# Feed-forward matmuls as pairs on two 64-row tiles, in a fused attention and gated feed-forward kernel

## The chip, the cores and the metric

The kernel runs on one core of one Trainium2 chip. The metric is device time in microseconds (us), the median of several executions.

Engine names in the profile: PE is TensorE, PEld its weight loads, DVE VectorE, ACT ScalarE, POOL GpSimd, SP the engine whose queue issues most of the DMAs.

## The reference

```
attention: 8 batches, 16 query heads, 4 key/value heads, 384 positions, head size 64
  a = softmax(q k^T / 8);  x = a v,  laid out as [batch, 384, 1024]
feed-forward with a spatial gate:
  h = relu(x @ w_in)                 # 1024 -> 1024
  u, v = halves of h                 # 512 each
  v_n = (v - mean) / sqrt(var + 1e-6)
  v_s = w_spatial @ v_n + b_spatial  # along the 384 positions
  out = (u * v_s) @ w_out            # 512 -> 1024
```

## The kernel before

The kernel is a software pipeline over the eight batches. While batch b has its scores and exps and v chunks 0 and 1, batch b-1 has v chunk 2, its spatial and u chunks and o (output) chunk 0, and batch b-2 has o chunks 1 to 5. The order on every engine is the order of the program.

- A *score unit* is two matmuls on two 64-row tiles of TensorE, since the head size is 64, and one exp over 1024 columns. 18 units make a batch.
- A *value* (three per batch) is 36 matmuls on four 32-column tiles.
- *v*, *u*, *sp* (spatial) and *o* (output) chunks are ordinary matmuls with 128 rows: 3 v chunks of 8 matmuls, 4 u of 8, 4 sp of 3, 6 o of 4 per batch. TensorE writes their sums into PSUM; four of its banks are used in rotation, and in this program the next chunk waits until VectorE or ScalarE has read its bank out.

```
def score_mm(b, u):
    for half in range(2):
        lo, hi = half * D, (half + 1) * D          # D = 64
        nc.tensor.matmul(sc[:, half, :], kT[b][lo:hi, gp, t, :], rhs[lo:hi, :], start=True, stop=True)

def u_mm(b, mu):
    pu = ps.tile([P, 512], FP32, ...)              # four PSUM banks in rotation
    for kc in range(NKT):
        nc.tensor.matmul(pu[:, 0:S], w_in16[:, kc, mu*P:(mu+1)*P], xT[b][:, kc, :], ...)

def visit(b, vi):                                  # nine visits per batch
    score_mm(b, 2*vi); score_mm(b, 2*vi + 1)
    exp(b, 2*vi)
    ...
    if vi == 4:
        norm(c); exp(b, u1)
        o_mm(d, 5); o_copy(d, 5)                   # the copy is followed by the store, on SP's queue
        v_mm(b, 0); relu(b, 0); stats(b, 0)
    ...

def next_loads(b, vi):                             # b is the next batch here
    if vi == 0: ...                                # loads on SP, casts on GpSimd
    if vi == 5: dma_transpose_k(b); dma_transpose_q(b, 0)
    if vi == 6: dma_transpose_q(b, 1)
```

The keys and queries of the next batch are transposed by DMAs from SBUF to SBUF, which SP issues.

The softmax here doesn't subtract the row's maximum and nothing guards it: scores larger than these inputs give would overflow.

Of the kernel before, what the change touches and what calls it, by code (L numbers as in the profile page):

```python
# [10 lines left out]
FP32 = mybir.dt.float32  # L11
# [8 lines left out]
def kernel(  # L20
# [20 lines left out]
    P = 128  # L41
# [23 lines left out]
    att_a = ctx.enter_context(tc.tile_pool(name="att_a", bufs=2))  # L65
# [8 lines left out]
    ps = ctx.enter_context(tc.tile_pool(name="ps", bufs=4, space=bass.MemoryType.PSUM))  # L74
# [13 lines left out]


# [102 lines left out]
    def transpose_ws(st):  # L192
        ws16 = loaded["ws16"]
        psw = ps.tile([P, NST, P], FP16, name=f"psw_{st}", tag="ps")
        for tt in range(NST):
            nc.tensor.transpose(psw[:, tt, :], ws16[:, tt, st, :], ident16)
        nc.vector.tensor_copy(wsT16[:, st, :].rearrange("p (t q) -> p t q", t=NST), psw)
# [23 lines left out]
    def transpose_k(b, gp):  # L221
        k16 = loaded["k16", b]
        pk = ps.tile([P, NST, P], FP16, name=f"pk_{b}_{gp}", tag="ps")
        for t in range(NST):
            nc.tensor.transpose(pk[:, t, :], k16[:, gp, t, :, :].rearrange("p h d -> p (h d)"), ident16)
        if b not in kT:
            new_kT(b)
        nc.vector.tensor_copy(kT[b][:, gp], pk)

    def transpose_q(b, gp, qt):  # L230
        q16 = loaded["q16", b, gp]
        if (b, gp) not in qT:
            new_qT(b, gp)
        pq = ps.tile([P, G, P], FP16, name=f"pq_{b}_{gp}_{qt}", tag="ps")
        for j in range(G):
            nc.tensor.transpose(  # L236
                pq[:, j, :], q16[:, qt, j, :, :].rearrange("p h d -> p (h d)"), ident16
            )
        nc.vector.tensor_copy(qT[b, gp][:, qt], pq)  # L239
# [4 lines left out]
    def score_mm(b, u):  # L244
        qt, gp, t = u // 6, (u % 6) // 3, u % 3
        sc = ps_sc.tile([P, 2, 512], FP32, name=f"sc_{b}_{u}", tag="sc")
        rhs = qT[b, gp][:, qt].rearrange("p j q -> p (j q)")
        for half in range(2):
            lo, hi = half * D, (half + 1) * D
            nc.tensor.matmul(  # L250
                sc[:, half, :], kT[b][lo:hi, gp, t, :], rhs[lo:hi, :], start=True, stop=True
            )
        held["sc", b, u] = sc
# [7 lines left out]
    def value_mm(b, qt):  # L261
# [15 lines left out]
        sums = ps.tile([P, 512], FP32, name=f"sums_{b}_{qt}", tag="ps")  # L277
        tiles(sums, lambda t, g: ones32)
        held["sums", b, qt] = sums
        for jj in range(2):  # L280
            X = ps.tile([P, 512], FP32, name=f"X_{b}_{qt}_{jj}", tag="ps")
            tiles(X, lambda t, g: v16[:, g, t, 32 * jj : 32 * (jj + 1)])
            held["X", b, qt, jj] = X

# [20 lines left out]
    def v_mm(b, st):  # L305
        pv = ps.tile([P, 512], FP32, name=f"pv_{b}_{st}", tag="ps")
# [45 lines left out]
    def sp_mm(b, m, dst=None):  # L352
        if dst is None:
            dst = ps.tile([P, 512], FP32, name=f"psp_{b}_{m}", tag="ps")
# [20 lines left out]
    def u_mm(b, mu):  # L375
        pu = ps.tile([P, 512], FP32, name=f"pu_{b}_{mu}", tag="ps")
# [22 lines left out]
    def o_mm(b, i):  # L399
        tt, half = i // 2, i % 2  # L400
        po = ps.tile([P, 512], FP32, name=f"po_{b}_{tt}_{half}", tag="ps")
# [26 lines left out]


# [76 lines left out]
    def next_loads(b, vi):  # L506
        if vi == 0:
            load_k(b)
            load_q(b, 0)
            load_q(b, 1)  # L510
            load_v(b)
            for gp in range(NGP):
                cast_k(b, gp, nc.gpsimd)
            for gp in range(NGP):
                for half in range(2):
                    cast_q(b, gp, 0, NST, half, nc.gpsimd)
            cast_v(b, nc.gpsimd)
        if vi == 5:
            dma_transpose_k(b)
            dma_transpose_q(b, 0)  # L520
        if vi == 6:
            dma_transpose_q(b, 1)

    def visit(b, vi):
        c, d = b - 1, b - 2
        u0, u1 = 2 * vi, 2 * vi + 1
        score_mm(b, u0)
        score_mm(b, u1)
        exp(b, u0)
        if vi == 0:  # L530
            value_mm(c, 2)
            rec(c, 2)
            exp(b, u1)
            xmul(c, 2)
            if d >= 0:
                o_mm(d, 1)
                o_copy(d, 1)
        if vi == 1:
            exp(b, u1)
            if d >= 0:  # L540
                for i in (2, 3):
                    o_mm(d, i)
                    o_copy(d, i)
            else:
                for gp in range(NGP):
                    transpose_q(1, gp, 1)
                v_mm(0, 1)
                relu(0, 1)
                stats(0, 1)
        if vi == 2:  # L550
            exp(b, u1)
            v_mm(c, 2)
            relu(c, 2)
            stats(c, 2)
            if d < 0:
                for gp in range(NGP):
                    transpose_q(1, gp, 2)
                cast_ws()
        if vi == 3:
            value_mm(b, 0)  # L560
            rec(b, 0)
            exp(b, u1)
            rstd(c)
            xmul(b, 0)
            if d >= 0:
                o_mm(d, 4)
                o_copy(d, 4)
            else:
                for st in range(NST):
                    transpose_ws(st)  # L570
        if vi == 4:
            norm(c)
            exp(b, u1)
            if d >= 0:
                o_mm(d, 5)
                o_copy(d, 5)
            v_mm(b, 0)
            relu(b, 0)
            stats(b, 0)
        if vi == 5:  # L580
            exp(b, u1)
            for m in range(NDT):
                sp_mm(c, m)
                sp_add(c, m)
            u_mm(c, 0)
            gate(c, 0)
        if vi == 6:
            value_mm(b, 1)
            rec(b, 1)
            exp(b, u1)  # L590
            xmul(b, 1)
            u_mm(c, 1)
            gate(c, 1)
        if vi == 7:
            exp(b, u1)
            for mu in (2, 3):
                u_mm(c, mu)
                gate(c, mu)
        if vi == 8:
            exp(b, u1)  # L600
            v_mm(b, 1)
            relu(b, 1)
            stats(b, 1)
            o_mm(c, 0)
            o_copy(c, 0)

    def tail():
        c, d = B - 1, B - 2
        value_mm(c, 2)
        rec(c, 2)  # L610
        rstd(c, 0, 2)
        xmul(c, 2)
        for i in (1, 2):
            o_mm(d, i)
            o_copy(d, i)
        norm(c, 0, 2)
        v_mm(c, 2)
        relu(c, 2)
        stats(c, 2)
        rstd(c, 2, 3)  # L620
        norm(c, 2, 3)
        for i in (3, 4, 5):
            o_mm(d, i)
            o_copy(d, i, nc.scalar)
# [16 lines left out]
    with tc.manual_schedule(engines={PE, POOL, SP, DVE, ACT}):  # L641
        first_batch()
        for b in range(1, B):
            for vi in range(VISITS):
                visit(b, vi)
                if b + 1 < B:
                    next_loads(b + 1, vi)
        tail()
# [29 lines left out]
```

## Time and profile before

265.06 us (three runs, 265.05 to 265.34).

| what | read from | value |
|---|---|---|
| PE busy share | the page | 94% |
| one batch in the steady part | timeline, from value to value | 29.47 us |
| 512-column matmul, start to start | instruction starts | 0.216 us |
| 384-column matmul, start to start | instruction starts | 0.162 us |
| extra gap where the tiling mode changes | instruction starts | 0.093 to 0.106 us, and 0.01 behind it |

The head of the page of the kernel before: busy us, share of the span, number of instructions. Below it is the head of the part on the chain that ended last.

```profile
span 262.5 us, 4805 instructions
PE 245.9 (94%) x1957; PEld 103.2 (39%) x1957; DVE 140.6 (54%) x261; ACT 187.3 (71%) x241; POOL 43.6 (17%) x69
...
PE 86%; ACT 8%; DVE 2%; DMA 1%; issue 0%; ACTq 0%
```

A piece of the timeline of the kernel before. Columns: start in us, duration in us, engine, line, operation, result <- inputs, tile rows*columns, shapes, number of instructions merged.

```profile
121.63 0.60 PE L250 MATMUL sc<-qT,kT 64*128 64x512 f16 x4
...
122.17 1.90 PE L403 MATMUL po<-w_out,gT 128*128 128x512 f16 x8
...
124.00 0.60 PE L250 MATMUL sc<-qT,kT 64*128 64x512 f16 x4
```

Compare starts, not durations, because matmuls are pipelined. From 122.17 to 124.00 eight matmuls pass: 8 x 0.216 = 1.73, and 0.10 more for the change back to the scores' mode. From 121.63 to 122.17 there are two pairs, 2 x 0.22 and again 0.10. Counted over a batch: 27.26 us of matmul slots (24 v + 24 o + 27 value + 18 score slots of 0.216; 32 u + 12 sp of 0.163) and 21 mode changes of about 0.10. That leaves almost nothing of the 29.47.

The DMA transposes of the kernel before, in the same view (SPq is SP's queue, the duration is that of the issue), and the first score of the batch that needs them:

```profile
104.03 1.40 SPq L209 DMA_TRANSPOSE kT<-k  x1
105.53 3.94 SPq L216 DMA_TRANSPOSE qT<-q  x2
...
118.07 0.61 PE L250 MATMUL sc<-qT,kT 64*128 64x512 f16 x4
```

The last of them had landed at 111.7 by the DMA's completion events, over six us before the score.

### The profile page before, as it was taken

The numbers are of one execution on the slowest core, as the hardware profiler recorded it, in microseconds if no ns is written. First come the engines' busy times: TensorE is split into PE (matmuls) and PEld (weight loads), VectorE is DVE, ScalarE is ACT, GpSimd is POOL, SyncE is SP. The second block draws the span as 40 slices with busy tenths as digits, with TensorE's granted clock in tenths as the row PEclk, the third lists the DMA queues.
The fourth block names the chain that finished last, engine by engine and source line by source line (L and its number), as shares of the span: only waits on it lengthen the run. The fifth ranks groups of instructions, "written<-read, shape, count | busy, mean of one in ns | idle before, by whom it ended". The sixth has DMA issues, their size and how long they took to land.

```text
span 262.5 us, 4805 instructions
## 1 busy us (share of the span) xinstructions
PE 245.9 (94%) x1957; PEld 103.2 (39%) x1957; DVE 140.6 (54%) x261; ACT 187.3 (71%) x241; POOL 43.6 (17%) x69
## 2 busy tenths in 40 slices
PE   2787798999999999999999999999999999999794
PEld 1233343443344333443344333443344333444351
DVE  2326649626493356626483457636483457637452
ACT  2889888667957888668957888668957888663301
POOL 2707422000160014100330016000330000000000
PEclk9999999999999999999999999999999999999998
DMA  8999999931997069902994079902985031002306
GB/s 185 283 254 352 275 230 74 172 14 60 303 263 128 0 215 340 198 2 70 305 278 100 4 217 339 195 0 76 314 264 100 2 160 54 28 0 84 160 0 240
DMA packets 57430, 41.60 MB, mean 158 GB/s; under 512 B 26816, under 2 KB 53568, under 8 KB 57408
## 3 DMA queue, kind: packets, MB, share of 16 engines
q1 hardware_dynamic: 53648, 37.89, 54.1%
q0 software_dynamic: 2720, 3.15, 8.4%
q10 hardware_dynamic: 1040, 0.26, 0.4%
q8 instruction: 15, 0.25, 0.4%
q14 instruction: 7, 0.06, 0.1%
HBM read 25.95 MB, written 12.58 MB: 147 GB/s over the span
## 4 chain that ended last, share of the span: by engine, by line
PE 86%; ACT 8%; DVE 2%; DMA 1%; issue 0%; ACTq 0%
PE po L403 17%; PE pu L378 16%; PE pv L308 16%; PE sc L250 14%; PE X L269 10%; PE sums L269 7%; ACT aT L259 6%; PE psp L356 5%; DMA q<-in_q_dram 1%; DVE v_s L368 1%; ACT rec L288 1%; PE sc_sp L356 1%; ACT rec L287 1%; PE pq L236 1%; DVE qT L239 1%; DVE ws L187 1%
## 5 line engine op out<-in xcount | busy, mean ns | idle before, releaser
L259 ACT ACTIVATE aT<-sc 128x1024 f16<-128x1024 f32 x144 | 140.8, 1019 | 40.9 <-PE sc L250 40.9
L250 PE MATMUL sc<-qT,kT 64*128 64x512 f16 x288 | 46.6, 394 | 5.7 <-ACT aT L259 4.4
L296 DVE TENSOR_TENSOR xt<-X,rec 128x512 f16<-128x512 f32 x48 | 30.9, 686 | 32.3 <-PE X L269 25.4
L403 PE MATMUL po<-w_out,gT 128*128 128x512 f16 x192 | 47.4, 380 | 0.0
L308 PE MATMUL pv<-w_in,xt 128*128 128x512 f16 x192 | 45.5, 380 | 0.0
L378 PE MATMUL pu<-xt,w_in 128*128 128x384 f16 x256 | 45.5, 327 | 0.0
L329 DVE BATCH_NORM_STATS2 stats<-v_r 128x6 f32<-128x512 f32 x24 | 16.7, 694 | 39.4 <-ACT v_r L322 39.3
L269 PE MATMUL X<-aT,v 128*32 128x512 f16 x576 | 35.5, 381 | 0.0
L421 DVE COPY osb<-po 128x512 f32<-128x512 f32 x42 | 28.6, 683 | 7.1 <-PE po L403 7.1
L378 PEld LDWEIGHTS <-w_in 128*128 128x128 f16 x256 | 23.9, 98 | 20.8 <-issue 5.9
L159 POOL CAST q<-q 128x768 f16<-128x768 f32 (+2 forms) x32 | 24.2, 785 | 41.4 <-DMA q<-in_q_dram 31.2
L390 DVE SCALAR_TENSOR_TENSOR gT<-pu,v_s 128x384 f16<-128x384 f32 x32 | 17.8, 558 | 17.6 <-PE pu L378 16.5
L308 PEld LDWEIGHTS <-xt 128*128 128x128 f16 x192 | 17.4, 98 | 25.0 <-issue 6.4
L403 PEld LDWEIGHTS <-gT 128*128 128x128 f16 x192 | 16.6, 98 | 26.2 <-issue 9.3
L250 PEld LDWEIGHTS <-kT 64*128 64x128 f16 x288 | 10.7, 94 | 34.3 <-issue 30.4
L140 POOL CAST k<-k 128x384 f16<-128x384 f32 x13 | 6.3, 507 | 106.5 <-issue 63.7
L269 PEld LDWEIGHTS <-v 128*32 128x32 f16 x576 | 15.5, 98 | 16.1 <-issue 0.8
L322 ACT ACTIVATE v_r<-pv 128x512 f32<-128x512 f32 x23 | 13.7, 597 | 11.4 <-PE pv L308 9.9
L269 PE MATMUL sums<-aT,ones 128*32 128x512 f16 x288 | 20.6, 393 | 0.0
L368 DVE TENSOR_TENSOR v_s<-psp,bias_b 128x384 f32<-128x384 f32 x28 | 16.7, 663 | 0.0
L287 ACT ACTIVATE rec<-sums 128x512 f32<-128x512 f32 x24 | 14.4, 599 | 2.2 <-PE sums L269 2.2
L288 ACT ACTIVATE rec<-rec 128x512 f32<-128x512 f32 x24 | 15.1, 630 | 0.8
(36 smaller groups left out, 102.4 us busy)
## 6 DMA issues: line engine op xcount, KB each, us to landing
out_dram<-osb SPq DMA_DIRECT2D x23, 512.0 KB, 3.3
q<-in_q_dram SPq DMA_DIRECT2D x14, 768.0 KB, 8.4
v<-in_v_dram SPq DMA_DIRECT2D x8, 384.0 KB, 9.0
k<-in_k_dram SPq DMA_DIRECT2D x7, 384.0 KB, 4.2
w_in<-in_moe_w_in_dram POOLq DMA_DIRECT2D x8, 256.0 KB, 8.9
q<-in_q_dram SPq DMA_DIRECT2D x2, 512.0 KB, 6.2
w_out<-in_moe_w_out_dram POOLq DMA_DIRECT2D x2, 512.0 KB, 20.2
ws<-in_moe_w_spatial_dram SPq DMA_DIRECT2D x1, 576.0 KB, 9.9
```

Source lines behind the costliest of these rows:

```text
L159: engine.tensor_copy(dst, src)
L250: nc.tensor.matmul(sc[:, half, :], kT[b][lo:hi, gp, t, :], rhs[lo:hi, :], start=True, stop=True)
L259: nc.scalar.activation(aT[b, qt][:, gp, t], held["sc", b, u], AF.Exp, scale=scale)
L269: nc.tensor.matmul(dst[32 * g : 32 * (g + 1), :], weights(t, g), a[:, g // 2, t, g % 2, :], start=(t == 0), stop=(t == NST - 1),)
L288: nc.scalar.activation(r, r, AF.Exp, scale=-1.0)
L296: nc.vector.tensor_tensor(xt[:, jj, :, qt * P : (qt + 1) * P], held["X", b, qt, jj].rearrange("p (j q) -> p j q", j=G), held["rec", b, qt] ...
L308: nc.tensor.matmul(pv, xT[b][:, kc, st * P : (st + 1) * P], w_in16[:, kc, DH:DFF], start=(kc == 0), stop=(kc == NKT - 1),)
L368: nc.vector.tensor_tensor(held["v_s", b][:, m, :].rearrange("p (t s) -> p t s", t=NST), held["psp", b, m][:, 0:S].rearrange("p (t s) -> p ...
L378: nc.tensor.matmul(pu[:, 0:S], w_in16[:, kc, mu * P : (mu + 1) * P], xT[b][:, kc, :], start=(kc == 0), stop=(kc == NKT - 1),)
L390: nc.vector.scalar_tensor_tensor(held["gT", b][:, mu, :], held["pu", b, mu][:, 0:S], 0.0, held["v_s", b][:, mu, :], op0=ALU.max, op1=ALU.mult,
L403: nc.tensor.matmul(po, held["gT", b][:, m, tt * P : (tt + 1) * P], w_out16[:, m, half * 512 : (half + 1) * 512], start=(m == 0), stop=(m = ...
L421: nc.vector.tensor_copy(osb[:, cols], held["po", b, i])
```

## The change

The intent is to take away the mode changes between scores and feed-forward chunks. Each chunk's contraction over 128 rows is cut into rows 0 to 63 and rows 64 to 127. Two chunks A and B then run together. In phase 1 the lower half of A and the upper half of B run in pairs on the two row tiles, into two different banks. In phase 2 the other halves follow. The Trainium skill, "TensorEngine Tiling (Array Packing)", Gotcha 1, says that different row tiles cannot access the same PSUM bank at the same time and that software must see to it. So phase 2 must not start before phase 1 is complete: GpSimd writes a one-element *mark* after the last matmul of phase 1, and the first matmul of phase 2 waits for the mark. Score units run in between as cover.

```diff
+    def passed(last):
+        done = nc.gpsimd.memset(mark, 0.0)
+        sync(done, last)
+        return done
+
+    def group_uu(b, m0, m1, between, banks=(None, None)):
+        last = pairs(u_part(b, m0, LO, banks[0]), u_part(b, m1, HI, banks[1]))
+        done = passed(last)
+        between()                                       # score units
+        pairs(u_part(b, m1, LO), u_part(b, m0, HI), after=done)
+        gate(b, m0)
+        gate(b, m1)
+    # group_sp: four sp chunks; group_voo: one v chunk against two o chunks
 ... (cut)
+    def batch(b, p, q, r, s):                           # p..s: the four banks
+        group_uu(d, 2, 3, units(1, 3), (r, s))
+        if more: cast_all_k(b + 1)                      # casts on GpSimd, spread
+        unit(b, 3); value(c, 2, (p, q, r)); unit(b, 4); xmul(c, 2)
+        group_voo(c, 1, d, 0, 1, units(5, 7), ...)      # first o/v group
 ... (cut)
+        group_voo(b, 0, d, 4, 5, units(13, 15), (p, s, r))   # third o/v group
+        if more: dma_transposes(b + 1)
+        if b + 2 < B: load_all(b + 2)
+        p, q, r, s = q, s, p, r
+        group_sp(c, (units(15, 16), units(16, 17)), (p, q, r, s))
+        def between():
+            unit(b, 17)
+            if more: unit(b + 1, 0)                     # first score of the next batch
+        group_uu(c, 0, 1, between, (p, q))
```

Batches 2 to 7 run like this. Batch 1 has an order of its own. The work of a batch is shifted: v chunk 1, u chunks 2 and 3 and o chunk 0 now come one batch later, and the tail after the last batch is longer by two u chunks, a v and an o.

The change has side effects. It moves most of the relus of v from ScalarE to VectorE (17 of 24 now run there, 1 of 24 before), it gives the exp results a third buffer, and it chooses the four banks by hand.

More of the change, by code (lines that the diff above doesn't have):

```diff
@@ L64 @@
     tr_sb = ctx.enter_context(tc.tile_pool(name="tr_sb", bufs=3))
-    att_a = ctx.enter_context(tc.tile_pool(name="att_a", bufs=2))
+    att_a = ctx.enter_context(tc.tile_pool(name="att_a", bufs=3))
     xt_pool = ctx.enter_context(tc.tile_pool(name="xt_pool", bufs=3))
@@ L73 @@
     ps_sc = ctx.enter_context(tc.tile_pool(name="ps_sc", bufs=2, space=bass.MemoryType.PSUM))
-    ps = ctx.enter_context(tc.tile_pool(name="ps", bufs=4, space=bass.MemoryType.PSUM))
+    ps = ctx.enter_context(tc.tile_pool(name="ps", bufs=1, space=bass.MemoryType.PSUM))
     need_funcs = {AF.Exp, AF.Relu, AF.Copy, AF.Identity, AF.Ln}
@@ L87, with bank @@
     )
+    turn = [0]
+    def bank(shape, dtype, name, i=None):
+        if i is None:
+            i = turn[0]
+        turn[0] = (i + 1) % 4
+        return ps.tile(shape, dtype, name=name, tag=f"ps{i}")
     loaded = {}
@@ L193, in transpose_ws @@
         ws16 = loaded["ws16"]
-        psw = ps.tile([P, NST, P], FP16, name=f"psw_{st}", tag="ps")
+        psw = bank([P, NST, P], FP16, f"psw_{st}")
         for tt in range(NST):
@@ L222, in transpose_k @@
         k16 = loaded["k16", b]
-        pk = ps.tile([P, NST, P], FP16, name=f"pk_{b}_{gp}", tag="ps")
+        pk = bank([P, NST, P], FP16, f"pk_{b}_{gp}")
         for t in range(NST):
@@ L233, in transpose_q @@
             new_qT(b, gp)
-        pq = ps.tile([P, G, P], FP16, name=f"pq_{b}_{gp}_{qt}", tag="ps")
+        pq = bank([P, G, P], FP16, f"pq_{b}_{gp}_{qt}")
         for j in range(G):
@@ L249, in score_mm @@
             lo, hi = half * D, (half + 1) * D
-            nc.tensor.matmul(
+            mm = nc.tensor.matmul(
                 sc[:, half, :], kT[b][lo:hi, gp, t, :], rhs[lo:hi, :], start=True, stop=True
             )
+            if half == 0:
+                held["score_mm"] = mm
         held["sc", b, u] = sc
@@ L259, in exp, with value_mm @@
         nc.scalar.activation(aT[b, qt][:, gp, t], held["sc", b, u], AF.Exp, scale=scale)
-    def value_mm(b, qt):
+    def value_mm(b, qt, banks=(None, None, None)):
         a = aT[b, qt]
@@ L275, in tiles @@
                     )
-        sums = ps.tile([P, 512], FP32, name=f"sums_{b}_{qt}", tag="ps")
+        sums = bank([P, 512], FP32, f"sums_{b}_{qt}", banks[0])
         tiles(sums, lambda t, g: ones32)
@@ L280, in value_mm @@
         for jj in range(2):
-            X = ps.tile([P, 512], FP32, name=f"X_{b}_{qt}_{jj}", tag="ps")
+            X = bank([P, 512], FP32, f"X_{b}_{qt}_{jj}", banks[1 + jj])
             tiles(X, lambda t, g: v16[:, g, t, 32 * jj : 32 * (jj + 1)])
@@ L305, in v_mm @@
     def v_mm(b, st):
-        pv = ps.tile([P, 512], FP32, name=f"pv_{b}_{st}", tag="ps")
+        pv = bank([P, 512], FP32, f"pv_{b}_{st}")
         for kc in range(NKT):
@@ L353, in sp_mm @@
         if dst is None:
-            dst = ps.tile([P, 512], FP32, name=f"psp_{b}_{m}", tag="ps")
+            dst = bank([P, 512], FP32, f"psp_{b}_{m}")
         for st in range(NST):
@@ L375, in u_mm @@
     def u_mm(b, mu):
-        pu = ps.tile([P, 512], FP32, name=f"pu_{b}_{mu}", tag="ps")
+        pu = bank([P, 512], FP32, f"pu_{b}_{mu}")
         for kc in range(NKT):
@@ L400, in o_mm @@
         tt, half = i // 2, i % 2
-        po = ps.tile([P, 512], FP32, name=f"po_{b}_{tt}_{half}", tag="ps")
+        po = bank([P, 512], FP32, f"po_{b}_{tt}_{half}")
         for m in range(NDT):
@@ L426, in o_copy, with v_part @@
             nc.sync.dma_start(rows, osb)
+    LO, HI = slice(0, D), slice(D, P)
+    def v_part(b, st, rows, at=None):
+        if ("pv", b, st) not in held:
+            held["pv", b, st] = bank([P, 512], FP32, f"pv_{b}_{st}", at)
+        first = held.setdefault(("pv_rows", b, st), rows) is rows
+        for kc in range(NKT):
+            yield lambda kc=kc: nc.tensor.matmul(
+                held["pv", b, st],
+                xT[b][rows, kc, st * P : (st + 1) * P],
+                w_in16[rows, kc, DH:DFF],
+                start=(first and kc == 0),
+                stop=(not first and kc == NKT - 1),
+            )
@@ new lines, in u_part @@
+    def u_part(b, mu, rows, at=None):
+        if ("pu", b, mu) not in held:
+            held["pu", b, mu] = bank([P, 512], FP32, f"pu_{b}_{mu}", at)
+        first = held.setdefault(("pu_rows", b, mu), rows) is rows
+        for kc in range(NKT):
+            yield lambda kc=kc: nc.tensor.matmul(
+                held["pu", b, mu][:, 0:S],
+                w_in16[rows, kc, mu * P : (mu + 1) * P],
+                xT[b][rows, kc, :],
+                start=(first and kc == 0),
+                stop=(not first and kc == NKT - 1),
+            )
@@ new lines, in sp_part @@
+    def sp_part(b, m, rows, at=None):
+        if ("psp", b, m) not in held:
+            held["psp", b, m] = bank([P, 512], FP32, f"psp_{b}_{m}", at)
+        first = held.setdefault(("psp_rows", b, m), rows) is rows
+        for st in range(NST):
+            yield lambda st=st: nc.tensor.matmul(
+                held["psp", b, m][:, 0:S],
+                held["v_n", b, st][rows, m * P : (m + 1) * P],
+                wsT16[rows, st, :],
+                start=(first and st == 0),
+                stop=(not first and st == NST - 1),
+            )
@@ new lines, in o_part @@
+    def o_part(b, i, rows, at=None):
+        tt, half = i // 2, i % 2
+        if ("po", b, i) not in held:
+            held["po", b, i] = bank([P, 512], FP32, f"po_{b}_{tt}_{half}", at)
+        first = held.setdefault(("po_rows", b, i), rows) is rows
+        for m in range(NDT):
+            yield lambda m=m: nc.tensor.matmul(
+                held["po", b, i],
+                held["gT", b][rows, m, tt * P : (tt + 1) * P],
+                w_out16[rows, m, half * 512 : (half + 1) * 512],
+                start=(first and m == 0),
+                stop=(not first and m == NDT - 1),
+            )
@@ new lines, with sync, unit, pairs @@
+    mark = cst.tile([1, 1], FP32, name="mark")
+    def sync(later, earlier):
+        tc.add_manual_dep(
+            later.ins,
+            earlier.ins.name,
+            mybir.DependencyInfo(mybir.DependencyClass.Sync, mybir.DependencyReason.DATA),
+            reason="other row tile, same bank",
+        )
+    def unit(b, u):
+        score_mm(b, u)
+        exp(b, u)
+    def pairs(lo, hi, behind=None, after=None):
+        lo, hi = list(lo), list(hi)
+        assert len(lo) == len(hi)
+        for n, (x, y) in enumerate(zip(lo, hi)):
+            i = x()
+            if n == 0 and after is not None:
+                sync(i, after)
+            i = y()
+            for what in (behind or {}).get(n + 1, ()):
+                what()
+        return i
@@ new lines, in passed, with group_sp @@
+    def passed(last):
[9 more added lines that the diff above has]
+        gate(b, m1)
+    def group_sp(b, between, banks=(None,) * 4):
+        done = {}
+        for m in (0, 2):
+            last = pairs(sp_part(b, m, LO, banks[m]), sp_part(b, m + 1, HI, banks[m + 1]))
+            done[m] = passed(last)
+            if m == 0:
+                between[0]()
+        for m in (0, 2):
+            pairs(sp_part(b, m + 1, LO), sp_part(b, m, HI), after=done[m])
+            sp_add(b, m)
+            sp_add(b, m + 1)
+            if m == 0:
+                between[1]()
@@ new lines, in group_voo @@
+    def group_voo(bv, st, bo, i0, i1, between, banks, mid=(), relu_on=None, voo=True):
+        last = pairs(
+            v_part(bv, st, LO, banks[0]),
+            [*o_part(bo, i0, HI, banks[1]), *o_part(bo, i1, HI, banks[2])],
+            {4: mid[:1]},
+        )
+        done = passed(last)
+        between()
+        pairs(
+            [*o_part(bo, i0, LO), *o_part(bo, i1, LO)],
+            v_part(bv, st, HI),
+            {4: [lambda: o_copy(bo, i0), *mid[1:]]},
+            after=done,
+        )
+        relu(bv, st, relu_on)
+        o_copy(bo, i1)
+        stats(bv, st)
@@ L432, with group_oo, value @@
+    def group_oo(b, i0, i1, between, banks=(None, None)):
+        last = pairs(o_part(b, i0, LO, banks[0]), o_part(b, i1, HI, banks[1]))
+        done = passed(last)
+        between()
+        pairs(o_part(b, i1, LO), o_part(b, i0, HI), after=done)
+        o_copy(b, i0)
+        o_copy(b, i1)
+    def value(b, qt, banks=(None, None, None)):
+        value_mm(b, qt, banks)
+        rec(b, qt)
     VISITS = 9
@@ L504, in first_batch @@
                     transpose_q(1, gp, 0)
-    def next_loads(b, vi):
-        if vi == 0:
-            load_k(b)
-            load_q(b, 0)
-            load_q(b, 1)
-            load_v(b)
-            for gp in range(NGP):
-                cast_k(b, gp, nc.gpsimd)
-            for gp in range(NGP):
-                for half in range(2):
-                    cast_q(b, gp, 0, NST, half, nc.gpsimd)
-            cast_v(b, nc.gpsimd)
-        if vi == 5:
-            dma_transpose_k(b)
-            dma_transpose_q(b, 0)
-        if vi == 6:
-            dma_transpose_q(b, 1)
@@ L524, in visit @@
-    def visit(b, vi):
-        c, d = b - 1, b - 2
-        u0, u1 = 2 * vi, 2 * vi + 1
-        score_mm(b, u0)
-        score_mm(b, u1)
-        exp(b, u0)
-        if vi == 0:
-            value_mm(c, 2)
-            rec(c, 2)
-            exp(b, u1)
-            xmul(c, 2)
-            if d >= 0:
-                o_mm(d, 1)
-                o_copy(d, 1)
-        if vi == 1:
-            exp(b, u1)
-            if d >= 0:
-                for i in (2, 3):
-                    o_mm(d, i)
-                    o_copy(d, i)
-            else:
-                for gp in range(NGP):
-                    transpose_q(1, gp, 1)
-                v_mm(0, 1)
-                relu(0, 1)
-                stats(0, 1)
-        if vi == 2:
-            exp(b, u1)
-            v_mm(c, 2)
-            relu(c, 2)
-            stats(c, 2)
-            if d < 0:
-                for gp in range(NGP):
-                    transpose_q(1, gp, 2)
-                cast_ws()
-        if vi == 3:
-            value_mm(b, 0)
-            rec(b, 0)
-            exp(b, u1)
-            rstd(c)
-            xmul(b, 0)
-            if d >= 0:
-                o_mm(d, 4)
-                o_copy(d, 4)
-            else:
-                for st in range(NST):
-                    transpose_ws(st)
-        if vi == 4:
-            norm(c)
-            exp(b, u1)
-            if d >= 0:
-                o_mm(d, 5)
-                o_copy(d, 5)
-            v_mm(b, 0)
-            relu(b, 0)
-            stats(b, 0)
-        if vi == 5:
-            exp(b, u1)
-            for m in range(NDT):
-                sp_mm(c, m)
-                sp_add(c, m)
-            u_mm(c, 0)
-            gate(c, 0)
-        if vi == 6:
-            value_mm(b, 1)
-            rec(b, 1)
-            exp(b, u1)
-            xmul(b, 1)
-            u_mm(c, 1)
-            gate(c, 1)
-        if vi == 7:
-            exp(b, u1)
-            for mu in (2, 3):
-                u_mm(c, mu)
-                gate(c, mu)
-        if vi == 8:
-            exp(b, u1)
-            v_mm(b, 1)
-            relu(b, 1)
-            stats(b, 1)
-            o_mm(c, 0)
-            o_copy(c, 0)
@@ new lines, in load_all, with cast_all_k, cast_all_q, dma_transposes @@
+    def load_all(b):
+        load_k(b)
+        load_q(b, 0)
+        load_q(b, 1)
+        load_v(b)
+    def cast_all_k(b):
+        for gp in range(NGP):
+            cast_k(b, gp, nc.gpsimd)
+    def cast_all_q(b, gp):
+        for half in range(2):
+            cast_q(b, gp, 0, NST, half, nc.gpsimd)
+    def dma_transposes(b):
+        dma_transpose_k(b)
+        dma_transpose_q(b, 0)
+        dma_transpose_q(b, 1)
+    def second_batch():
+        one = [lambda u=u: unit(1, u) for u in range(18)]
+        def v_full(b, st):
+            v_mm(b, st)
+            relu(b, st, nc.vector)
+            stats(b, st)
+        one[0]()
+        one[1]()
+        value(0, 2)
+        one[2]()
+        for gp in range(NGP):
+            transpose_q(1, gp, 1)
+        xmul(0, 2)
+        v_full(0, 1)
+        one[3]()
+        load_all(2)
+        cast_all_k(2)
+        cast_all_q(2, 0)
+        cast_all_q(2, 1)
+        cast_v(2, nc.gpsimd)
+        one[4]()
+        v_full(0, 2)
+        one[5]()
+        for gp in range(NGP):
+            transpose_q(1, gp, 2)
+        cast_ws()
+        one[6]()
+        value(1, 0)
+        rstd(0)
+        one[7]()
+        xmul(1, 0)
+        norm(0)
+        for st in range(NST):
+            transpose_ws(st)
+        one[8]()
+        v_full(1, 0)
+        one[9]()
+        one[10]()
+        group_sp(0, one[11:13])
+        value(1, 1)
+        one[13]()
+        xmul(1, 1)
+        dma_transposes(2)
+        load_all(3)
+        def between():
+            one[14]()
+            one[15]()
+        group_uu(0, 0, 1, between)
+        v_full(1, 1)
+        one[16]()
+        one[17]()
+        unit(2, 0)
@@ new lines, in batch, with units, between @@
+    def batch(b, p, q, r, s):
+        c, d = b - 1, b - 2
+        more = b + 1 < B
+        def units(u0, u1):
+            def between():
+                for u in range(u0, u1):
+                    unit(b, u)
+            return between
+        group_uu(d, 2, 3, units(1, 3), (r, s))
+        if more:
+            cast_all_k(b + 1)
+        unit(b, 3)
+        value(c, 2, (p, q, r))
+        unit(b, 4)
+        xmul(c, 2)
+        if b == 2:
+            group_oo(d, 0, 1, units(5, 7), (s, p))
+            unit(b, 7)
+        else:
+            group_voo(c, 1, d, 0, 1, units(5, 7), (s, p, q), (lambda: None, units(7, 8)), nc.vector)
+        if more:
+            cast_all_q(b + 1, 0)
+        value(b, 0, (r, p, s))
+        unit(b, 8)
+        xmul(b, 0)
+        group_voo(c, 2, d, 2, 3, units(10, 12), (q, r, p), (units(9, 10),), nc.vector)
+        if more:
+            cast_all_q(b + 1, 1)
+        value(b, 1, (s, r, q))
+        unit(b, 12)
+        rstd(c)
+        xmul(b, 1)
+        norm(c)
+        if more:
+            cast_v(b + 1, nc.gpsimd)
+        group_voo(b, 0, d, 4, 5, units(13, 15), (p, s, r))
+        if more:
+            dma_transposes(b + 1)
+        if b + 2 < B:
+            load_all(b + 2)
+        p, q, r, s = q, s, p, r
+        group_sp(c, (units(15, 16), units(16, 17)), (p, q, r, s))
+        def between():
+            unit(b, 17)
+            if more:
+                unit(b + 1, 0)
+        group_uu(c, 0, 1, between, (p, q))
+        return p, q, r, s
@@ L607, in tail @@
     def tail():
         c, d = B - 1, B - 2
-        value_mm(c, 2)
-        rec(c, 2)
-        rstd(c, 0, 2)
-        xmul(c, 2)
-        for i in (1, 2):
-            o_mm(d, i)
-            o_copy(d, i)
-        norm(c, 0, 2)
+        for mu in (2, 3):
+            u_mm(d, mu)
+            gate(d, mu)
+        value(c, 2)
+        xmul(c, 2)
+        v_mm(c, 1)
+        relu(c, 1, nc.vector)
+        stats(c, 1)
+        rstd(c, 0, 2)
+        o_mm(d, 0)
+        o_copy(d, 0, nc.scalar)
         v_mm(c, 2)
@@ L618, in tail @@
         relu(c, 2)
+        norm(c, 0, 2)
         stats(c, 2)
@@ L621, in tail @@
         norm(c, 2, 3)
-        for i in (3, 4, 5):
+        for i in range(1, 6):
             o_mm(d, i)
@@ L642 @@
         first_batch()
-        for b in range(1, B):
-            for vi in range(VISITS):
-                visit(b, vi)
-                if b + 1 < B:
-                    next_loads(b + 1, vi)
+        second_batch()
+        banks = 0, 1, 2, 3
+        for b in range(2, B):
+            banks = batch(b, *banks)
         tail()
```

## The prediction

> **What bounds the kernel now.** TensorE. The page has PE busy 94%, and the chain of waits puts 86% of the span on PE lines. In the steady part (batches 2 to 7) the timeline repeats every 29.47 us (value sums at 78.72, 108.20, 137.67). Start-to-start times: a 512-column matmul 0.216 us, a 384-column one 0.162, a pair of score matmuls on two 64-row tiles 0.22 per pair (starts 3 ns apart). One batch streams about 27.2 us: v 24, o 24 and values 27 slots of 0.216, u 32 and sp 12 of 0.162, scores 18 pairs. The rest is mode changes: wherever scores, values and 128-row matmuls meet, the gap is 0.31 instead of 0.216, plus 0.01 behind it. 21 such changes of about 0.103 are 2.2 us; 27.2 + 2.2 is the period. The Trainium skill, TensorEngine Tiling (Array Packing), Key Properties, says that a change of tiling mode drains the engine; the trace agrees, at 0.10 us each.
>
> **Removed.** All feed-forward work of batches 2 to 7 goes to the scores' mode; only three values per batch still change mode: 6 changes instead of 21, about 1.55 us per batch, 9 us in all.
>
> **Added.** Twice the feed-forward instructions (PE queue only) and seven GpSimd marks per batch. A mark needs the 0.16 us tail of the last matmul, a memset of about 0.1 and two semaphores, some 0.4 to 0.5 us, covered by two score units (0.44): 0 to 0.15 us of wait each.
>
> **Moved, and decisive.** Before, the transposing DMAs for the next batch start some 10 us before their first use. After, the queue issues them behind the output store of o chunk 5, which waits for the last o/v group; the first score unit of the next batch now stands inside the u group of this batch. Chain from the last matmul of the o/v group: matmul tail 0.17, copy 0.68, store issue 0.45, then from the issue of the k transpose to the landing of the first q transpose 5.2 to 6.0 (the DMA events of before: 5.9 to 6.2 beside loads). Together about 6.9 us (6.5 to 7.3). TensorE has only 3.9 us of work there (sp group, half a u group, three score units). From that score unit to the end of the next o/v group it has 24.0 us, 24.2 to 25 with marks. These two close a cycle: period about 31.4 instead of 29.47, though the streamed work would allow 27.9.
>
> The second batch sheds two u chunks and an o, batch 2 a v, but the tail gets those 5.2 us back.
>
> **Sum.** First unit of batch 2 near 55.5; batch 3 near 84; then four periods of 31.4 to 209.5; last o/v group ends near 234; tail from 240; span near 271.5, time 274 us. Range 266 to 281.
>
> **Signs.** Right if: mode-change gaps only around values; half-matmul pairs every 0.216 (0.162 for u, sp); in the waits, PE's weight load for a score behind the transposing DMA, about 2 to 3 us, once per batch, five times, and the chain of waits running through output copy, store queue and transposes; period above 30.5.
>
> **Wrong if:** transposes land within 4 us of the o/v group's end (then about 255 to 258); pairs run below one slot per pair; marks cost over 0.3 us each; or the TensorE gaps lower the granted clock (slower still).
>
> Chances: faster by over 2% 0.09, within 2% 0.19, slower by over 2% 0.72.

## The result, and the profile after

278.91 us (four runs, 278.1 to 279.1) against 265.2 us in the same rounds. The ratio is 1.0509, interval 1.0486 to 1.0533. The change is 5% slower.

The head of the page and of the chain, kernel after:

```profile
span 276.8 us, 6011 instructions
PE 247.0 (89%) x2529; PEld 116.2 (42%) x2529; DVE 150.0 (54%) x274; ACT 183.7 (66%) x228; POOL 47.9 (17%) x114
...
PE 78%; DMA 8%; DVE 6%; ACT 5%; issue 1%; SPq 0%; POOLq 0%; POOL 0%; ACTq 0%
```

PE is busy for nearly the same time (247.0 us against 245.9) in a longer span, and 8% of the chain is now DMA. From the view of who waited for whom (total us, times, longest):

```profile
PE sc L259 <- DMA qT<-q: 8.6, 5, 2.7
PE sc L259 <- ACT aT L270: 4.7, 10, 0.9
PEld L491 <- POOL mark L528: 4.6, 11, 0.5
PE pu L464 <- DVE v_s L379: 1.5, 6, 0.3
```

The first line is the new wait: five times, once for every batch whose keys and queries come by DMA within this loop. Here is one of them in the timeline of the kernel after, engine by engine. First PE, from the last pairs of the third o/v group:

```profile
142.66 0.38 PE L491 MATMUL po<-w_out,gT 64*128 64x512 f16 x1
142.66 0.38 PE L451 MATMUL pv<-w_in,xt 64*128 64x512 f16 x1
142.88 0.72 PE L477 MATMUL psp<-wsT,v_n 64*128 64x384 f16 x6
...
145.71 0.32 PE L464 MATMUL pu<-xt,w_in 64*128 64x384 f16 x1
146.29 1.46 PE L464 MATMUL pu<-xt,w_in 64*128 64x384 f16 x15 [0.26 <-DVE v_s L379]
147.44 0.52 PE L259 MATMUL sc<-qT,kT 64*128 64x512 f16 x2
149.69 0.39 PE L259 MATMUL sc<-qT,kT 64*128 64x512 f16 x2 [1.73 <-DMA qT<-q]
```

Then the copy of o chunk 5 on DVE, and SP's queue:

```profile
143.07 0.69 DVE L432 COPY osb<-po 128x512 f32<-128x512 f32 x1 [0.17 <-PE pv L451]
...
143.79 0.34 SPq L437 DMA_DIRECT2D out_dram<-osb  x1
144.23 1.40 SPq L218 DMA_TRANSPOSE kT<-k  x1
146.17 2.99 SPq L225 DMA_TRANSPOSE qT<-q  x2
```

Last pair at 142.66, copy at 143.07, store at 143.79, key transpose at 144.23, query transposes from 146.17, score at 149.69: 7.03 us. In the five batches this stretch was 6.80, 6.69, 7.03, 6.67 and 7.95 us. From that score to the last pair of the next third o/v group it was 24.38 or 24.39 us each time. The sum of the two is the period: 31.1, 31.4, 31.1 and 32.3 us between the values of consecutive batches, against 29.47 before. (The chain view names a mark as what released the key transpose of this batch; the queue shows that its issue began at 144.23, before that mark at 144.58. Releasers are inferred.)

The pairs themselves do what was intended: in the o/v groups the two halves start a few ns apart, and the pairs follow each other at 0.2155 us, one full matmul's time. Extra gaps of 0.10 stand only around the values.

### The profile page after: what moved, and what is told of

It is laid out like the page before. It is cut to its first block, busy times and chain, and to the rows that moved or that the text cites. A ratio compares the mean times of both kernels' runs of the same rounds, so it can differ in the third digit from the quotient of the medians.

```text
span 276.8 us, 6011 instructions
## 1 busy us (share of the span) xinstructions
PE 247.0 (89%) x2529; PEld 116.2 (42%) x2529; DVE 150.0 (54%) x274; ACT 183.7 (66%) x228; POOL 47.9 (17%) x114
## 4 chain that ended last, share of the span: by engine, by line
PE 78%; DMA 8%; DVE 6%; ACT 5%; issue 1%; SPq 0%; POOLq 0%; POOL 0%; ACTq 0%
PE sc L259 12%; PE po L491 11%; PE pv L451 11%; PE X L280 11%; PE pu L464 10%; DMA qT<-q 7%; PE sums L280 6%; PE psp L477 5%; ACT aT L270 4%; PE pv L319 4%; PE po L414 4%; PE pu L389 3%; DVE v_s L379 2%; DMA q<-in_q_dram 1%; DVE v_n L353 1%
## 5 line engine op out<-in xcount | busy, mean ns | idle before, releaser
L259 PE MATMUL sc<-qT,kT 64*128 64x512 f16 x288 | 55.0, 392 | 14.9 <-DMA qT<-q 8.6
L491 PE MATMUL po<-w_out,gT 64*128 64x512 f16 x288 | 68.1, 376 | 0.0
L451 PE MATMUL pv<-w_in,xt 64*128 64x512 f16 x272 | 66.0, 376 | 0.0
L464 PE MATMUL pu<-xt,w_in 64*128 64x384 f16 x416 | 39.3, 323 | 2.0 <-DVE v_s L379 1.5
L259 PEld LDWEIGHTS <-kT 64*128 64x128 f16 x288 | 17.2, 94 | 43.7 <-issue 32.8
L491 PEld LDWEIGHTS <-gT 64*128 64x128 f16 x288 | 25.5, 94 | 16.6 <-POOL mark L528 4.6
L451 PEld LDWEIGHTS <-xt 64*128 64x128 f16 x272 | 24.7, 94 | 14.1
L464 PEld LDWEIGHTS <-w_in 64*128 64x128 f16 x416 | 22.2, 94 | 17.2 <-issue 5.0
L477 PE MATMUL psp<-wsT,v_n 64*128 64x384 f16 x168 | 18.7, 322 | 0.2 <-DVE wsT L206 0.2
L331 DVE TENSOR_SCALAR v_r<-pv 128x512 f32<-128x512 f32 x17 | 11.7, 691 | 9.5 <-PE pv L319 5.4
```

Of the source, the lines that this page charges most:

```text
L259: mm = nc.tensor.matmul(sc[:, half, :], kT[b][lo:hi, gp, t, :], rhs[lo:hi, :], start=True, stop=True)
L451: yield lambda kc=kc: nc.tensor.matmul(held["pv", b, st], xT[b][rows, kc, st * P : (st + 1) * P], w_in16[rows, kc, DH:DFF], start=(first a ...
L464: yield lambda kc=kc: nc.tensor.matmul(held["pu", b, mu][:, 0:S], w_in16[rows, kc, mu * P : (mu + 1) * P], xT[b][rows, kc, :], start=(firs ...
L477: yield lambda st=st: nc.tensor.matmul(held["psp", b, m][:, 0:S], held["v_n", b, st][rows, m * P : (m + 1) * P], wsT16[rows, st, :], start ...
L491: yield lambda m=m: nc.tensor.matmul(held["po", b, i], held["gT", b][rows, m, tt * P : (tt + 1) * P], w_out16[rows, m, half * 512 : (half ...
```

## The experiments

Nine further kernels ran. Times are medians of fast runs. "Period" is the distance between the last values of consecutive batches, in the steady part of each run's trace.

| run | us | before | ratio (interval) | period, us |
|---|---|---|---|---|
| after | 278.91 | 265.2 | 1.0509 (1.0486 to 1.0533) | 31.1 to 32.3 |
| e1_early | 268.93 | 265.26 | 1.0140 (1.0118 to 1.0163) | 29.53 |
| e2_use_later | 274.87 | 265.26 | 1.0408 (1.0344 to 1.0473) | 29.7 to 32.0 |
| e3_full_rows | 269.84 | 265.26 | 1.0186 (1.0161 to 1.0211) | 30.01 |
| e4_steady | 268.43 | 264.88 | 1.0138 (1.0113 to 1.0163) | 29.30 |
| e5_all | 267.47 | 264.88 | 1.0095 (1.0067 to 1.0123) | 29.11 |
| e6_tail | 264.94 | 264.88 | 1.0003 (0.9982 to 1.0024) | 29.11 |
| e7_before_tail | 263.17 | 264.88 | 0.9942 (0.9920 to 0.9964) | 29.47 |
| e8_light_dve, one look | 264.24 | 264.46 | none | 28.39 |
| e9_light_both, one look | 276.96 | 264.46 | none | 28.23 |

Theory A is the prediction's: the late transposes close a cycle. Rival B: marks and half-row pairs cost more than the mode changes that they remove.

### e1_early: the transposes ahead of the store

```diff
-        group_voo(b, 0, d, 4, 5, units(13, 15), (p, s, r))
         if more:
             dma_transposes(b + 1)
+        group_voo(b, 0, d, 4, 5, units(13, 15), (p, s, r))
```

> The changed kernel with one call moved: the transposing DMAs of the next batch are issued before the third o/v group of the batch instead of after it, so that the queue has them ahead of the output store of o chunk 5. Theory A (the late transposes are the whole loss): the waits of a score for a transposing DMA (five, 8.6 us in the trace, 1.7 to 3.0 each) vanish, the period falls from 31.1-32.3 to 28 to 28.6 us, and the time falls by about 15 us to 262 to 265, that is, level with the kernel before or a little better. Rival B (marks on GpSimd and half-row pairs cost more than the removed mode changes, and the transposes hide behind that): only 0 to 5 us come back, time 274 to 279.

268.93 us: 10.0 us come back by moving one call. No score waits for a transpose any more. In SP's queue (timeline of e1_early) the transposes now start 5.4 us before the store of o chunk 5, the last line here:

```profile
104.42 1.39 SPq L218 DMA_TRANSPOSE kT<-k  x1
105.91 3.15 SPq L225 DMA_TRANSPOSE qT<-q  x2
109.80 0.43 SPq L437 DMA_DIRECT2D out_dram<-osb  x1
```

So the late transposes are 10.0 of the 13.7 us lost; the other 3.7 us stay. Rival B as put, 0 to 5 us, is out. But theory A expected 15 us: the period fell to 29.53, not to 28 or 28.6. Something else fills the room of the mode changes, and the waits for the transposes had hidden it. One piece of it is in the timeline of e1_early:

```profile
110.99 2.41 DVE L379 TENSOR_TENSOR v_s<-psp,bias_b 128x384 f32<-128x384 f32 x4 [0.34 <-PE psp L477]
110.95 0.71 PE L477 MATMUL psp<-wsT,v_n 64*128 64x384 f16 x6
111.73 0.32 PE L464 MATMUL pu<-xt,w_in 64*128 64x384 f16 x1
112.30 0.99 PE L464 MATMUL pu<-xt,w_in 64*128 64x384 f16 x10 [0.25 <-DVE v_s L379]
```

The u group uses the banks of sp chunks 0 and 1. Each is free only when DVE has added the bias, 0.67 us a chunk. The two halves of the first pair start at 111.73 and 112.30, where PE could have gone on at 111.45 (the last pair of the spatial group starts at 111.28). VectorE itself waited 0.34 us for TensorE before these adds, so this wait is not a queue of the relus that were moved to it.

### e2_use_later: the first use moved by half a u group

```diff
-        def between():
-            unit(b, 17)
-            if more:
-                unit(b + 1, 0)
-        group_uu(c, 0, 1, between, (p, q))
+        group_uu(c, 0, 1, units(17, 18), (p, q))
+        if more:
+            unit(b + 1, 0)
```

> The changed kernel, transposes left where they are, but the first score unit of the next batch stands behind the whole u group of this batch instead of in its middle: its use is 1.3 us of TensorE work later. Theory A (cycle of output copy, store, transposes, score): each of five waits shrinks by about 1.3 us and one score unit fewer covers the mark of that group (about 0.2 us back): time falls by 5 to 6 us, to 272.5 to 274. Rival B: nothing changes or it gets slower by 1 us, 279 to 280.

274.87 us, 4.0 less than the changed kernel. Its four runs scatter from 274.05 to 277.99; the two profiled executions, at clocks 1.00 and 0.999, are 4.05 apart (274.05 and 278.1). The waits of scores for the transposes shrank from 8.6 us in five to 3.2 us in two, 5.4 less:

```profile
PE sc L259 <- DMA qT<-q: 3.2, 2, 2.1
```

This is the direction of theory A, with the gain 1 us short of the 5 to 6 expected. Where in the order the first use stands is thus a lever too, but as tried here a weaker one than the start of the DMA: 4.0 us against 10.0.

### e3_full_rows: the new order without half rows

```diff
 def group_uu(b, m0, m1, between, banks=(None, None)):
-    last = pairs(u_part(b, m0, LO, banks[0]), u_part(b, m1, HI, banks[1]))
-    done = passed(last)
+    at_bank(banks[0])
+    u_mm(b, m0)
     between()
-    pairs(u_part(b, m1, LO), u_part(b, m0, HI), after=done)
+    at_bank(banks[1])
+    u_mm(b, m1)
     gate(b, m0)
     gate(b, m1)
 # the other groups likewise; transposes early as in e1_early
```

> As e1_early (transposes early), but the grouped feed-forward chunks run as full 128-row matmuls again, each chunk in one piece, without half-row pairs and without marks; order of chunks and scores nearly as in e1_early. Theory A: about 15 more mode changes of 0.10 us per batch come back, minus what the marks cost: 1.2 to 1.6 us per batch, so 7 to 10 us slower than e1_early, with mode-change gaps of 0.31 us again around the scores. Rival B (half-row pairs cost as much as they save): within 2 us of e1_early or faster.

269.84 us, only 0.9 above e1_early instead of 7 to 10. Theory A missed here, and the time is what rival B of this run forecast (half-row pairs cost as much as they save: within 2 us). The traces show where the saving went. That of e3_full_rows has 26 mode changes per batch in its steady part, and next to nothing else between the slots (27.26 + 26 x 0.103 = 29.9 of 30.01). A score unit between full chunks costs two changes:

```profile
135.82 0.39 PE L259 MATMUL sc<-qT,kT 64*128 64x512 f16 x2
136.14 1.90 PE L319 MATMUL pv<-w_in,xt 128*128 128x512 f16 x8
137.97 0.39 PE L259 MATMUL sc<-qT,kT 64*128 64x512 f16 x2
```

From 135.82 to 136.14 is 0.32, where 0.22 would do. e1_early has six changes, so 20 x 0.103 = 2.1 us per batch were taken out, and the period fell by 0.48. Read from instruction starts, a period of e1_early (29.53) is 27.26 of slots, 0.64 for the six changes, and these waits: 0.86 for banks that DVE had not read out (sp 0.17, u 0.69), 0.38 of two score units for ACT, 0.16 for a mark. 0.2 stay unattributed. The pairs themselves take one slot each. Most of what the mode changes gave back was taken by waits that do not stand in the period of e3_full_rows.

### e4_steady and e5_all: the new waits taken away

e4_steady runs score unit 17 before the u group and two units of the next batch inside it. e5_all also mends the order in batch 1, the banks of the first o pair in batch 2, the banks in the tail, and the place of unit 7.

```diff
+        unit(b, 17)
         def between():
-            unit(b, 17)
             if more:
                 unit(b + 1, 0)
+                unit(b + 1, 1)
 ... (later units moved up by one; e5_all, cut:)
-            group_oo(d, 0, 1, units(5, 7), (s, p))
+            group_oo(d, 0, 1, units(5, 7), (p, s))
```

> As e1_early, whose period is 29.53 us although its mode changes are down to six (0.64 us): in its trace the first pair of the u group waits 0.2 + 0.4 us per batch for the copies of the spatial group that free its two banks. Here one score unit (17) runs before that u group instead of inside it, and two score units of the next batch stand inside it, the later ones moved up by one. Theory C (waits for PSUM banks behind VectorE took the gain): about 0.2 to 0.4 us per batch come back, period 29.1 to 29.35, time 266.5 to 268. Rival D (the half-row pairs themselves are slow): period stays at 29.5, time 268.5 to 269.5.

> As e4_steady, and the other new waits of the change's own order taken away: in the second batch the attention product is multiplied before the query transposes are copied (a v chunk waited 1.2 us for it), the first o pair of batch 2 uses the banks in the order in which they are copied out (a value waited 0.6 us), the two u chunks of the tail take the banks that are free (0.8 us), score unit 7 one pair later (0.2 us per batch). Theory C: another 2 to 3.5 us, time 263.5 to 265.5, about level with the kernel before. Rival D: no change from e4_steady.

e4_steady: 268.43 us, period 29.30, within the expected range of the period and 0.4 us above that of the time. Its time against e1_early is from another chip and differs by less than the runs scatter, and the ratios are alike (1.0138 and 1.0140); only the period shows a gain. e5_all: 267.47 us, period 29.11. The period followed theory C, but 1 us instead of 2 to 3.5 came back.

### e6_tail and e7_before_tail: a wait of both kernels, and the control

In the tail the four spatial chunks share two tiles, so every second one waits for a copy. This was so in the kernel before as well. Both got the same edit:

```diff
         for m in range(NDT):
-            sp_mm(c, m, sc[m // 2][:, m % 2, :])
+            sp_mm(c, m, sc[m][:, 0, :] if m < 2 else None)
             sp_add(c, m)
```

> As e5_all, and in the tail the four spatial chunks use four tiles (two of the scores', two others) instead of halves of two, so that a chunk does not wait for the copy of the one before; these waits were in the kernel before too (0.9 and 1.0 us). Expected: 1.5 to 2 us less than e5_all, 262 to 264, slightly better than the kernel before.

> Control for e6_tail: the kernel before with that same edit of the tail alone. Expected 263.2 to 263.8, 1.5 to 2 us less than the kernel before. If e6_tail is not below this, the half-row pairs bring nothing even with their new waits taken away.

e6_tail is level with the kernel before (264.94 against 264.88), above the expected 262 to 264. e7_before_tail is at 263.17, and its interval lies below 1: the fastest kernel, 0.6% ahead of the kernel before and below e6_tail. By the test set beforehand, the pairs bring no time here. So with its new waits reduced, the change gains 0.36 us per steady batch (29.47 to 29.11), and still ends 1.8 us behind. How the loss splits between batch 1 and the tail stays open. Profiles of identical code differ by 1.3 us at the first value in batch 2 (59.7 in the kernel before, 61.0 in e7_before_tail), which is nearly as much as is to be explained.

### e8_light_dve and e9_light_both: wrong, for the period

```diff
-            held["v_s", b][:, m, :] ... psp[:, 0:S] ... bias_b        # 384 columns
+            held["v_s", b][:, m, 0:P], psp[:, 0:P], bias_b[:, 0:P]    # 128 columns
 # norm of v likewise 128 of 512 columns; e9 also: exp on half its columns
```

> Wrong result on purpose, for the period alone: as e6_tail (period 29.11 us in its trace), but the bias add of the spatial chunks and the norm of v work on 128 columns instead of 384 and 512 (the rest stays at a constant). Theory C (in the new order TensorE waits for VectorE's copies, and a mark waits for the norm): the wait of 0.41 us in the u group and the 0.16 us in front of the third o/v group's second phase vanish: period 28.5 to 28.7. Rival D (half-row pairs are slow in themselves): period stays within 0.1 of 29.1.

> Wrong result on purpose: as e8_light_dve, and every exp of the attention works on half its columns, so that ACT is lightly loaded. Theory C: the remaining 0.2 us wait of score unit 11 for ACT goes as well, period 28.0 to 28.4, near the 27.9 that the prediction counted from slots and six mode changes. Rival D: period stays above 28.6.

The period fell to 28.39 and then to 28.23 us. The pairs can thus run near the 27.9 that the prediction counted; no pair was touched, so it was the work of DVE, and by 0.16 us that of ACT, in the new order that kept e6_tail at 29.11. The starts of the last values of consecutive batches, in e6_tail and then in e8_light_dve:

```profile
118.18 0.83 PE L280 MATMUL sums<-aT,ones 128*32 128x512 f16 x12
147.30 0.83 PE L280 MATMUL sums<-aT,ones 128*32 128x512 f16 x12
```

```profile
120.82 0.83 PE L280 MATMUL sums<-aT,ones 128*32 128x512 f16 x12
149.21 0.83 PE L280 MATMUL sums<-aT,ones 128*32 128x512 f16 x12
```

No run lightened DVE in the kernel before; slots and mode changes fill 29.4 of its 29.47 us, so little could come back there. The results of both light runs still passed the comparison (the spatial weights are about 0.01/384 beside a bias of 1, and the scores are near 0), which says nothing for them as kernels. The time of e9_light_both is useless: memsets on DVE delay the first casts until 26.5 us, a fault of the experiment:

```profile
8.62 5.18 DVE L838 MEMSET aT_c<- 128x6144 f16 x1 [1.23 <-issue]
15.02 5.18 DVE L838 MEMSET aT_c<- 128x6144 f16 x1 [1.23 <-issue]
21.43 5.18 DVE L838 MEMSET aT_c<- 128x6144 f16 x1 [1.23 <-issue]
26.53 0.49 DVE L149 CAST k<-k 128x384 f16<-128x384 f32 x1
```

These runs also bear on a detail. In the changed kernel 39 of the 45 marks take 0.088 us, and the six that overlap the norm on DVE take 0.24. With the norm on 128 columns all 45 take 0.088 in e8_light_dve, and six take 0.126 in e9_light_both. All the stretched marks end 0.03 us after a norm instruction that had begun before them. The Trainium skill, "GPSIMD Engine Reference", Key points, says that GpSimd shares its SBUF interfaces with VectorE, with contention in some VectorE modes or when VectorE has two inputs in SBUF; the trace agrees in that a DVE instruction stretches a one-element memset by 0.15 us. Which mode the norm runs in, no run shows.

Whether the mark can be left out stays open.

## Why the prediction was right

It said 274 us (266 to 281), slower by over 2% with a chance of 0.72. The measured time is 278.91. Its terms:

| term | predicted | measured |
|---|---|---|
| pair of half matmuls | one slot, 0.216 | 0.2155 |
| mode changes left per batch | 6 | 6, all around values |
| end of third o/v group to first score | 6.9 us (6.5 to 7.3) | 6.45 to 7.73 (the stretches above less the last pair's slot) |
| first score to end of the next third o/v group | 24.2 to 25 us | 24.4 |
| issue of the key transpose to landing of the first query transpose | 5.2 to 6.0 us | 5.0 to 6.3 us |
| period | 31.4 us | 31.1, 31.4, 31.1, 32.3 |
| wait of that score for the DMA | 2 to 3 us at its weight load, five times | 2.1 us on average at the weight load, 1.7 at the matmul, longest 2.7; five times |
| mark | 0 to 0.15 us | mostly 0, 0.16 in the third o/v group |
| first unit of batch 2 | 55.5 us | 58.4 us |
| start of the tail | 240 us | 245 us |
| if the transposes came early | 255 to 258 us | 268.9 (e1_early), 264.9 with the other mends |

Two of the prediction's readings of the kernel before are a little off: its transposes start 14 us before their first use (104.03 to 118.07), not some 10, and from the issue of the keys to the landing of the first queries it took 5.65 to 7.09 us, not 5.9 to 6.2. Neither changes the sum.

- **Right, and shown by e1_early and e2_use_later:** what decides is the queue order of the transposes. They wait behind a store that waits for a copy, and the first score that needs them had been moved forward at the same time. Taking the five waits away returned 10.0 us.
- **Right:** the half-row pairs and the marks cost next to nothing by themselves (0.2155 us a pair; 0.16 us of wait for a mark per batch of e1_early).
- **Mis-sized:** the wait of the score is shorter than predicted because PE already stands 0.7 us in front of the u group for banks, within the same 6.9 us. The term for batch 1 was 2.9 us too small. In the trace of e1_early, where batch 1 is the same, a v chunk waits 1.2 us for the attention product; the rest was not taken apart. Between the last third o/v group and the tail another 1.3 us were not foreseen, of which two u chunks' wait for a gate is 0.65 (in the trace of e1_early).
- **Wrong:** "the streamed work would allow 27.9", and 255 to 258 us with early transposes. The sum held only PE slots, mode changes and marks. It left out that the same four banks must be read out by DVE and ACT within a shorter batch. e1_early, e3_full_rows, e8_light_dve and e9_light_both showed it: of 2.1 us removed per batch 1.6 came back, 1.4 of it in waits that the trace names.
- **Luck, in part:** the forecast held because the late transposes closed a longer loop, which covers most of the waits that were left out. Without the late transposes the same sum would have missed by 11 to 14 us and on the wrong side: it promised 3 to 4% less than the kernel before, and e1_early took 1.4% more.

The Trainium skill, "TensorEngine Tiling (Array Packing)", PSUM Bottleneck, says that "Tiling speeds up TensorE but not PSUM evacuation". The trace of e1_early agrees about the evacuation: 0.86 us per batch are waits for banks that were not read out. (Here the pairs were no faster than full matmuls; only the mode changes went.) The prediction should have drawn on that section too.

## What to carry to other kernels

When a change moves the consumer of a DMA earlier and its issue later, add up the whole loop from the last instruction that holds up the issue queue to the consumer and back: SP's queue issued in the order of the program here, so transposes that were ready stood behind a store that was not (143.79, then 144.23). When a bound engine is relieved, look for the next wait in line, which can take the gain (here mostly banks that VectorE must read out), and test it by making that engine's work lighter, wrong result or not. Give a control its share of every mend: the tail edit that brought the changed kernel level (2.5 us) made the old one faster too (1.7 us).

## What the Trainium skill lacked or had wrong

- "TensorEngine Tiling (Array Packing)", Key Properties: it says that a change of tiling mode drains TensorE, without a cost. The runs show 0.093 to 0.106 us per change and 0.01 at the next matmul, for 128-row, 64-row and 32-column modes alike.
- The same page, When to Use Tiling: for row tiling it names contractions of up to 64 only. Here a contraction of 128 rows cut in two halves on two row tiles ran at 0.2155 us per pair of 512 columns, as fast as the full matmul (0.216), with two weight loads per slot.
- The same page, Gotcha 1, asks for synchronization between row tiles on one bank, without its price. As done here a mark takes 0.088 us on GpSimd (0.24 beside the norm on DVE), and two score units cover its round trip but for up to 0.16 us.
- "DMA: Bandwidth & Descriptors", DMA Transpose (X-bar): no time from issue to landing of small SBUF-to-SBUF transposes on trn2. The kernel after shows, in batches 3 to 7, 1.4 us of issue for 6 tiles of 128x128, 1.4 to 2.3 us for 12, and for these 3.3 to 4.8 us from issue to landing. Together with the order of the queue this latency decided the case.
